# A pre-norm transformer block on one core: planner's places, warming products, the last attention unit and the closing sums of the last stage

## The chip, the cores and the metric

The kernel runs on one of the cores of a Trainium2 chip. The metric is the device time of one execution in microseconds (us). Besides the timed runs there is one profiled execution, whose trace the views of the profile are taken from. The core has five engines that each work through a list of their own in order: TensorE (PE; its weight loads are shown as PEld), VectorE (DVE), ScalarE (ACT), GpSimd (POOL) and SyncE (SP), which here only issues transfers. They wait for each other by semaphores.

## The reference

All is fp32. x has S = 2048 rows of D = 640; H = 32 heads of 20; F = 1728.

```python
x = A_x
h = x + attention(layernorm(x)) @ wo     # 32 heads, softmax over all 2048 keys, no mask
g = silu(layernorm(h) @ w_gate); u = layernorm(h) @ w_up
out = h + (g * u) @ w_down
```

Products are computed nearly exactly: each operand is split into a high part (type fp32r, one pass of PE) and a low part (the rest), and three of the four products of parts are added (`split`, L95 to L97: ScalarE rounds the high part, another engine subtracts).

## The kernel before, in words

**Start (to 17 us).** Four weight tiles and the first 512 rows of x are loaded. TensorE runs three fp32 products of no use as warming (L896 to L898), into a pair of banks that `ps_wide` (L80) takes in turn from three pairs (L74). VectorE normalises the rows (L755), TensorE transposes them (`flip_tokens`, L797) into pairs from the same turn, ScalarE and VectorE split them into z_hi and z_lo, and `first_blocks` (L819) multiplies the first two blocks of queries and keys into banks 0 and 1.

**Projections (to 336 us).** For four chunks c of 512 rows, ten blocks of queries and keys (`query_key`, two tiles of 128 columns a pair) and eight parts of values (`value`) are made. A product works on 64 rows, so that two of them, one in each half of the array, run side by side. In between stand row maxima of the attention scores that are computed early: score products against keys that have landed, with a maximum taken by VectorE. They give the largest score of each query, which the exponentials need. Two forms: `max_differences` (L200), two banks, where ScalarE writes the Relu of one half of the columns to a place in SBUF and VectorE adds and takes the maximum (L205, L207); and `max_twice` (L212), in two parts, where the first product's Relu is written to a place (L231) and the second product, issued later by the returned function, is added to it by VectorE (L224). The keys are first turned into differences by GpSimd (L431).

The order of all this is computed by the class `Halves` (L530) while the program is built. It keeps a modelled time for each half of PE, a time at which each engine is free (`use`), one for each of the eight banks (`places`), and issues what fits: `run` (L688) carries a block through both halves, `pair` (L605) puts in the next score product if a bank is free in the model, `finish_second` (L671) the second part of an open one. Before, each half can have one open product, and the three places for Relu (two halves of a spare query tile and a piece of v_stk, L512 to L520) are given out in rotation, whatever still reads them. `queries_at` (L994) is the modelled landing of a unit's queries, transfer plus 3.5 us. `raw_place` (L372) turns a weight tile that is no longer needed into a place for staged keys; ScalarE must once write it as fp32r from w_hi (L379), which `place` (L375) does; three of them are made at step 9 and one at step 6. `keep` (L833) splits a block and stores it.

**Attention (to 1476 us).** 32 units (8 groups of 4 heads, 4 chunks of queries) of 16 key tiles each. Per key tile TensorE makes four score products (`scores`, L1369), ScalarE four exponentials (L1380), and TensorE multiplies the probabilities by the values (`weigh`, L1382, eight instructions) one key tile later. A list `todo` holds the tiles whose weighing is due; a string of letters sets the order within a tile. In the last two units pieces of the output projection (`projection`, L1067) of the first two chunks are put in (`extra`): eight products of 128 x 320 (L1103), the moments, then four transposes (`flip`, L1128). By L1508 to L1510, unit 30 does the work of chunk 0 with whole rows (15 products of 128 rows), unit 31 that of chunk 1 with halved rows (`halved`, 30 products of 64 rows, into two banks, added by two operations of VectorE). In unit 31 the weighing is due two at a time on every second key tile up to tile 14 (L1472):

```python
both = u == NU - 1 and kt < NT - 1
for _ in range(2 * (1 - kt % 2) if both else 1):
    if todo:
        weigh_next()
```

**Feed-forward (to the end).** Two pairs of chunks, each over 14 blocks of F (`ELEMENTS`, L1342), by a Strassen-like scheme with seven instead of eight products. Element e runs in 6 or 8 steps (`step`); each step issues loads of weights from rings (`Ring`), some products of the down projection (`next_down`, L1646), prepares operands on GpSimd (`prepare`, `split` at L97, operand yp), and takes up to two `chores` (L2017). Chores are the closing sums of the scheme (`put_together`, L1673): 8 additions of 128 x 320 on GpSimd (L1684) for each of four token pairs of a pair of chunks. They have to be done before a token tile is stored; what is left of them then is issued at once (`plain`, L1687 to L1714). Elements 0 to 13 are of the first pair of chunks, 14 to 27 of the second, and the last blocks of the first pair's down projection run into elements 13 to 15. The last token tile is stored in two halves, both by SP (L1712).

## Time and profile before

| what | us |
|---|---|
| median of 3 runs | 2037.76 (2036.97 to 2040.04) |
| the profiled execution, its time | 2040.81 |
| its span, first to last instruction | 2039.0 |
| PE busy in the span | 2009.1 |
| VectorE, ScalarE, GpSimd busy | 1616.7, 1463.3, 778.5 |

"Busy" of PE is the union of modelled durations of its products, so a busy PE is not PE at its peak. The views used are the page (busy times, the chain of work that ended last), the table of windows (busy time by engine in stretches of the span, with the clock that TensorE was granted as a share of full speed), the list of waits (engine, line, what it waited for: us in total, times, longest), the groups by line, and the timeline (start, duration, engine, line, operation, tiles, number of instructions merged, and in brackets the idle time before and what ended it).

### The profile page before, as it was taken

The page shows a single profiled execution, that of the slowest core. Times are in us where ns is not written, and L with a number is a line of the kernel's source. Part 1 is how long each engine was busy: PE and PEld are TensorE (multiplying, and loading weights), DVE is VectorE, ACT ScalarE, POOL GpSimd, SP SyncE. Part 2 cuts the span into 40 slices and gives each one's busy share as a digit, 9 for nine tenths or more (in the row PEclk, how much of TensorE's full clock was granted, in tenths as well). Part 3 has the DMA queues.
Part 4 walks back from the last instruction along what each step waited for, and adds up shares of the span by engine and source line. Part 5 has one row for each costly group of instructions (what it writes and reads, how often), then busy time and mean ns, then how long its engine had stood idle before and what let it go on. Part 6 is the DMA issues. An engine that isn't in the chain of part 4 may idle for free.

```text
span 2039.0 us, 39356 instructions
## 1 busy us (share of the span) xinstructions
PE 2009.1 (99%) x13836; PEld 1244.3 (61%) x13836; DVE 1616.7 (79%) x3261; ACT 1463.3 (72%) x2948; POOL 778.5 (38%) x1075
## 2 busy tenths in 40 slices
PE   7999999999999999999999999999999999999998
PEld 6888897333333333333333333345598888888888
DVE  7769776888888888888888888886478666676677
ACT  4887887999999999999999999996634222212221
POOL 4464342234343434344430011001146454754555
PEclk9999999999999999999999999999999999999999
DMA  7775574343533534444433123211159654974642
GB/s 228 236 214 184 167 215 116 104 137 103 150 125 108 158 112 143 135 145 137 149 127 108 30 61 83 82 62 49 36 180 325 208 193 154 350 267 158 204 149 92
DMA packets 205206, 304.93 MB, mean 150 GB/s; under 512 B 47648, under 2 KB 82720, under 8 KB 203984
## 3 DMA queue, kind: packets, MB, share of 16 engines
q1 hardware_dynamic: 204912, 302.40, 45.6%
q8 instruction: 110, 1.80, 0.4%
q14 instruction: 88, 0.72, 0.1%
q10 hardware_dynamic: 96, 0.00, 0.0%
HBM read 205.78 MB, written 95.68 MB: 148 GB/s over the span
## 4 chain that ended last, share of the span: by engine, by line
PE 94%; DMA 2%; DVE 1%; ACT 1%; POOL 1%; issue 1%; SPq 0%; DVEq 0%; ACTq 0%; POOLq 0%
PE banks L1384 25%; PE banks L1374 17%; PE banks L1552 16%; PE banks L238 12%; PE banks L1646 8%; PE banks L569 8%; PE banks L1103 3%; PE banks L217 3%; PE banks L194 1%; DMA qk_d<-e 0%; PE banks L826 0%; PE banks L263 0%; DMA q_stk<-qk_d 0%; ACT q_stk L231 0%; DMA xt<-in_A_x 0%
## 5 line engine op out<-in xcount | busy, mean ns | idle before, releaser
L1380 ACT ACTIVATE probs<-banks 128x512 f32<-128x512 f32 x2048 | 1056.2, 614 | 61.1 <-PE banks L1374 25.3
L244 DVE TENSOR_REDUCE mx<-banks 128x1 f32<-128x512 f32 x1472 | 925.4, 684 | 124.9 <-PE banks L238 76.3
L1374 PE MATMUL banks<-q_stk,k_stk 62*128 62x512 f32 x2048 | 583.2, 428 | 1.5 <-ACT probs L1380 1.5
L1384 PE MATMUL banks<-probs,v_stk 128*32 128x512 f32 x4096 | 545.4, 606 | 0.0
L238 PE MATMUL banks<-k_stk,q_stk 60*128 60x512 f32 x1472 | 486.7, 438 | 0.2
L1374 PEld LDWEIGHTS banks<-q_stk,k_stk 62*128 62x128 f32 x2048 | 291.8, 184 | 283.7 <-ACT probs L1380 271.4
L238 PEld LDWEIGHTS banks<-k_stk,q_stk 60*128 60x128 f32 x1472 | 244.2, 184 | 163.1 <-DVE mx L244 126.8
L1769 DVE TENSOR_TENSOR tmp<-banks,tmp 128x512 f32<-128x512 f32 x208 | 141.2, 689 | 118.4 <-PE banks L1552 92.8
L1384 PEld LDWEIGHTS banks<-probs,v_stk 128*32 128x32 f32 x4096 | 81.3, 108 | 183.1 <-issue 171.4
L1646 PE MATMUL banks<-halves,yp 128*128 128x320 f32 x1032 | 178.9, 308 | 1.4 <-POOL yp L97 1.2
L1646 PEld LDWEIGHTS banks<-halves,yp 128*128 128x128 f32 x1032 | 165.2, 188 | 17.4 <-POOL yp L97 1.5
L1552 PE MATMUL banks<-t,units 128*128 128x512 f32 x624 | 162.7, 396 | 0.1
L97 POOL TENSOR_TENSOR yp<-y,yp 128x256 fp32r<-128x256 f32 x96 | 60.3, 628 | 195.2 <-ACT yp L96 181.0
L1552 PE MATMUL banks<-z,units 128*128 128x512 f32 x516 | 133.8, 394 | 0.0
L255 POOL CAST both<-neg 128x16 fp32r<-128x16 f32 x32 | 6.6, 206 | 314.7 <-PE banks L1374 138.2
L1552 PEld LDWEIGHTS banks<-t,units 128*128 128x128 f32 x624 | 112.5, 188 | 18.9 <-DVE tmp L1769 0.3
L1651 DVE TENSOR_TENSOR h<-banks,h 128x320 f32<-128x320 f32 x248 | 110.0, 481 | 6.8 <-PE banks L1646 5.4
L224 DVE CUSTOM_DVE_ANT_0 q_stk<-banks,q_stk 128x512 f32<-128x512 f32 x139 | 92.7, 687 | 26.0 <-PE banks L217 13.2
L569 PE MATMUL banks<-z_hi,w_hi 64*128 64x512 f32 x380 | 102.4, 406 | 1.9 <-ACT z_hi L96 1.8
L569 PE MATMUL banks<-z_lo,w_hi 64*128 64x512 f32 x380 | 103.3, 395 | 0.0
L1552 PEld LDWEIGHTS banks<-z,units 128*128 128x128 f32 x516 | 93.1, 187 | 16.1 <-DVE tmp L1769 0.2
L96 ACT ACTIVATE yp<-tmp 128x512 fp32r<-128x512 f32 x40 | 25.3, 632 | 103.2 <-POOL tmp L1639 103.2
(213 smaller groups left out, 2960.9 us busy)
## 6 DMA issues: line engine op xcount, KB each, us to landing
units<-w_d SPq DMA_DIRECT2D x186, 256.0 KB
w_d<-stage SPq DMA_DIRECT2D x106, 256.0 KB
halves<-j_d SPq DMA_DIRECT2D x70, 320.0 KB
k_stk<-qk_d SPq DMA_DIRECT2D x116, 160.0 KB
j_d<-stage SPq DMA_DIRECT2D x42, 320.0 KB
q_stk<-qk_d SPq DMA_DIRECT2D x64, 160.0 KB
k_stk<-qk_d SPq DMA_DIRECT2D x116, 80.0 KB
rb<-r_d SPq DMA_DIRECT2D x32, 256.0 KB
```

What stands on the lines that cost most here:

```text
L217: nc.tensor.matmul(ps, q[rows, pair, t * P : (t + 1) * P], k[rows, pair, :], start=True, stop=True)
L224: nc.vector.tensor_tensor_reduce(out=place, in0=ps, in1=place, scale=1.0, scalar=LEAST, op0=ALU.add, op1=ALU.max, accum_out=mx[:, b, pair, ...
L238: nc.tensor.matmul(ps, queries[u][rows, pair, t * P : (t + 1) * P], keys[u // NC][rows, pair, kc * CH : (kc + 1) * CH], start=True, stop=True,
L244: nc.vector.tensor_reduce(mxs[u][:, b, pair, t, kc : kc + 1], ps, axis=AX.X, op=ALU.max)
L569: product = nc.tensor.matmul(job["ps"][:, :out], lhs, rhs, start=(half == 0 and i == 0), stop=(half == 1 and i == job["n"] - 1),)
L1374: nc.tensor.matmul(ps, keys[u // NC][rows, p, kt * P : (kt + 1) * P], queries[u][rows, p, :], start=True, stop=True,)
L1380: nc.scalar.activation(probs[p][:, b, :], ps, AF.Exp, scale=scale)
L1384: nc.tensor.matmul(acc[32 * j : 32 * j + 32, :], values[u // NC][:, kt, j * VW : j * VW + 32], probs[j // 2][:, j % 2, :], start=(kt == 0) ...
L1552: nc.tensor.matmul(ps.rearrange("p (t n) -> p t n", t=TPC), w[k][:, i], z[k][:, :, j], start=(first and m == 0), stop=(last and m == len(n ...
L1646: nc.tensor.matmul(ps, a, b, start=(n == 0), stop=(n == len(pairs) - 1))
L1651: nc.vector.tensor_tensor(out=h, in0=ps, in1=h, op=ALU.add)
L1769: add = lambda out, ps, x: nc.vector.tensor_tensor(out=out, in0=ps, in1=x, op=ALU.add)
```

## The change

- The pairs of banks in turn are four (0, 2, 4, 6) instead of three; two warming products instead of three; the first blocks go to banks 2 and 3.
- The places for Relu have a modelled time each: `free_place` gives the one that is free first, or none, and then `pair` issues nothing. Each half may have two open products (`OPEN`).
- `raw_place` is written by VectorE, and may be used from the modelled end of that.
- Modelled times: ScalarE's two parts in `keep` 0.62 and 0.54 instead of 0.5 each; queries land 4.5 us after their transfer instead of 3.5.
- In the last unit two weighings on every second key tile only up to tile 9, one each from tile 10 on; the projection of chunk 1 has whole rows.
- The closing sums go one per step up to element 14, two after that.
- The first half of the last token tile is stored by ScalarE's queue.

```diff
-    wide_places, one_places = [2, 4, 6], []
+    wide_places, one_places = [0, 2, 4, 6], []
...
         def raw_place():
-            return place(raw_tile().rearrange("p a b -> p (a b)")[:, : 2 * CH], nc.scalar)
+            return place(raw_tile().rearrange("p a b -> p (a b)")[:, : 2 * CH], nc.vector)
...
-            if engine is nc.scalar:
+            if engine is nc.vector:
                 some = w_hi.rearrange("p k c -> p (k c)")[:, : 2 * CH].bitcast(F32)
-                nc.scalar.activation(t, some, AF.Copy)
-                pe.use("scalar", 1.0)
-                return t.rearrange("p (h n) -> p h n", h=2)
+                nc.vector.tensor_copy(t, some)
+                t = t.rearrange("p (h n) -> p h n", h=2)
+                place_at[id(t)] = pe.use("vector", 0.65) + 0.2
+                return t
...
-        def next_place():
-            relus.append(relus.pop(0))
-            return relus[-1]
+        relu_at = {}
+
+        def free_place(at):
+            place = min(relus, key=lambda r: relu_at.get(id(r), 0.0))
+            return place if relu_at.get(id(place), 0.0) <= at else None
...
-                self.second = [None, None]
+                self.second = [], []
...
-                if half is None and any(self.second) or half is not None and self.second[half]:
+                if half is None and any(self.second) or half is not None and len(self.second[half]) == OPEN:
                     return False
                 at = self.banks(1 if half is not None else 2)
                 if at is None:
                     return False
-                second = queue.pop(ahead)[1](at)
+                place = free_place(t + 0.43)
+                if place is None:
+                    return False
+                second = queue.pop(ahead)[1](at, place)
+                relu_at[id(place)] = math.inf
                 if half is not None:
                     start = self.stream(half, 0.231)
                     seen = self.use("scalar", 0.48, start + 0.43) + 0.2
                     self.places[at[0]] = seen
-                    self.second[half] = second, seen
+                    self.second[half].append((second, seen, place))
                     return True
...
                 for i, end in zip(at, ends):
                     self.places[i] = self.use("vector", 0.36, end) + 0.14
+                relu_at[id(place)] = self.places[at[1]]
                 return True
...
-                second, seen = self.second[half]
+                second, seen, place = self.second[half][0]
                 at = self.banks(1)
                 if at is None or self.now() + 0.43 < seen:
                     return False
-                self.second[half] = None
+                del self.second[half][0]
                 second(at)
                 start = self.stream(half, 0.231)
                 self.places[at[0]] = self.use("vector", 0.62, max(seen, start + 0.43)) + 0.14
+                relu_at[id(place)] = self.places[at[0]]
                 return True
...
-            pss = ps_at(range(2))
+            pss = ps_at((2, 3))
...
-                free = pe.use("scalar", 0.5, start)
-                done = pe.use("scalar", 0.5)
+                free = pe.use("scalar", 0.62, start)
+                done = pe.use("scalar", 0.54)
...
-        for _ in range(3):
+        for _ in range(2):
             nc.tensor.matmul(warm[:, 0], ident, xs[TPC - 1][:, :CH], start=True, stop=True)
...
-                    queries_at[u] = pe.sp(n=4, kb=750) + 3.5
+                    queries_at[u] = pe.sp(n=4, kb=750) + 4.5
...
-                    both = u == NU - 1 and kt < NT - 1
+                    both = u == NU - 1 and kt < NT // 2 + 2
...
                     ahead = projection(
-                        c - 1, ps_max if c < NC - 1 else (lambda: ps_b()), c == NC - 2
+                        c - 1, ps_max if c < NC - 1 else (lambda: ps_b())
                     )
...
-                nc.sync.dma_start(out[tt * P : (tt + 1) * P, cs], h_c[self.c][:, self.t + i, cs])
+                queue = nc.scalar if first and not half else nc.sync
+                queue.dma_start(out[tt * P : (tt + 1) * P, cs], h_c[self.c][:, self.t + i, cs])
...
-            for _ in range(2):
+            for _ in range(1 if e <= NF else 2):
                 if chores:
                     chores.pop(0)[2]()
```

More of the change, by code (lines that the diff above doesn't have):

```diff
@@ L41 @@
 MARGIN = 0.2
+OPEN = 2
 BEHIND = 2
@@ L452, in staged_keys, with one @@
                 all_products = [(t, pair, None) for t in range(TPC) for pair in range(2)]
-            def one(t, pair, b, at):
+            def one(t, pair, b, at, place):
                 rows = queries[u] if q is None else items[q][3]
                 if b is None:
-                    max_differences(mxs[u], rows, items[ks[0]][3], pair, t, kc, next_place(), at)
+                    max_differences(mxs[u], rows, items[ks[0]][3], pair, t, kc, place, at)
                     return over()
                 first, more = (items[k][3] for k in ks)
-                second = max_twice(mxs[u], rows, first, more, pair, t, kc, b, next_place(), at)
+                second = max_twice(mxs[u], rows, first, more, pair, t, kc, b, place, at)
                 return lambda at: (second(at), over())
@@ L482, in staged_keys @@
                     and (q is not None or pe.now() >= queries_at.get(u, math.inf)),
-                    lambda at, a=a: one(*a, at), a[2],
+                    lambda at, place, a=a: one(*a, at, place), a[2],
                 )
@@ L830, in first_blocks @@
             for m, ps in enumerate(pss):
-                pe.places[m] = keep(0, m, ps)
+                pe.places[2 + m] = keep(0, m, ps)
         def keep(c, m, ps):
```

## The prediction

> **What bounds the kernel now.** I read the page first, then a table of windows over the stages, then the waits of TensorE (PE), and the timeline only where PE waits.
>
> ```profile
> span 2039.0 us, 39356 instructions
> PE 2009.1 (99%) x13836; PEld 1244.3 (61%) x13836; DVE 1616.7 (79%) x3261; ACT 1463.3 (72%) x2948; POOL 778.5 (38%) x1075
> PE 94%; DMA 2%; DVE 1%; ACT 1%; POOL 1%; issue 1%; SPq 0%; DVEq 0%; ACTq 0%; POOLq 0%
> ...
> 13.00:325.00 312.00, 298.98 (x2744) 276.85 (x2744) 238.46 (x834) 247.29 (x537) 142.62 (x118) 0.98 0.65 201
> 1454.90:1476.40 21.50, 20.45 (x117) 7.54 (x113) 10.22 (x26) 14.76 (x29) 1.54 (x1) 0.92 0.00 1
> 1755.00:1795.00 40.00, 38.78 (x205) 33.99 (x204) 25.73 (x50) 7.41 (x15) 38.09 (x46) 1.00 0.99 369
> ```
>
> A row of windows gives stretch and length, then busy time of PE, weight loads, VectorE (DVE), ScalarE (ACT), GpSimd (POOL), then the granted clock. PE is nearly always busy and carries 94% of the chain, so only time in which PE stands still, or runs at a lower clock, can be won. Such time lies in four places: the first 17 us; the projections (13 of 312 us idle, clock 0.98); the last attention unit, whose closing 21.5 us have clock 0.92 and an ACT with 6.7 us to spare; and 1755 to 1795, where POOL is full and PE loses 1.2 us. The attention between has no edit.
>
> **Start: one warming product fewer, transposes spread over four pairs of banks.**
>
> ```profile
> 7.68 5.36 PE L898 MATMUL banks<-xt,ident 128*128 128x512 f32 x6 [7.68 <-DMA xt<-in_A_x]
> 11.07 1.66 DVE L755 TENSOR_SCALAR xt<-xt,mv,r_a 128x640 f32<-128x640 f32 x3
> 12.88 1.80 PE L801 MATMUL banks<-ident,xt 128*128 128x128 f32 x15
> 13.08 0.61 DVE L755 TENSOR_SCALAR xt<-xt,mv,r_a 128x640 f32<-128x640 f32 x1 [0.35 <-PE banks L898]
> 13.62 1.90 ACT L96 ACTIVATE z_hi<-banks 128x640 fp32r<-128x640 f32 x3 [2.86 <-PE banks L801]
> 15.24 0.77 PE L801 MATMUL banks<-ident,xt 128*128 128x128 f32 x5 [0.56 <-DVE z_lo L97]
> 16.80 2.58 PE L826 MATMUL banks<-z_hi,w_hi 128*128 128x512 f32 x10 [0.79 <-ACT z_hi L96]
> 5.98:9.39 3.41, 1.71 (x2) 0.84 (x3) 2.49 (x9) 0.00 (x0) 2.44 (x1) 1.00 1.04 363
> 9.39:12.80 3.41, 3.41 (x5) 1.25 (x4) 3.03 (x12) 1.36 (x2) 0.00 (x0) 1.00 1.10 350
> ```
>
> Three fp32 products are six instructions: (12.80 - 7.68) / 6 = 0.853 us each. Two products end at 11.1. The first tile is normalised at 11.07 + 0.55 = 11.6, so its transposes start near 11.8 instead of 12.88, and the fourth tile no longer waits 0.35 for the warming product that reads it. The fourth tile's transposes now go to banks 0 and 1, last used by the warming products, and lose the 0.56 behind VectorE. First conversion on ACT then at about 13.05; four of 0.63 follow without the present hole, so they end near 15.6 and L826 starts at 15.75 instead of 16.80: **1.0 us**. The first blocks' new banks 2 and 3 are those of the first tile, whose second part on DVE is over by 14.6: nothing. Bounds: 1.4 gained if the transposes are fast from their start, 1.7 lost if the clock rises later (a rival below).
>
> **Projections: the planner.** Here the order of instructions is computed from modelled times, and PE executes it strictly, so each wait is a place where the model was too early.
>
> ```profile
> PE banks L217 <- ACT q_stk L231: 4.3, 5, 1.6
> PE banks L217 <- ACT v_stk L231: 1.2, 1, 1.2
> PE banks L783 <- DVE mx L207: 1.7, 1, 1.7
> PE banks L194 <- DMA q_stk<-qk_d: 1.3, 2, 1.0
> ...
> 172.21 1.21 ACT L231 ACTIVATE q_stk<-banks 128x512 f32<-128x512 f32 x2 [1.98 <-DVE mx L224]
> 56.56 2.93 ACT L379 ACTIVATE raw<-w_hi 128x1024 fp32r<-128x1024 f32 x3
> 59.79 0.42 DVE L207 CUSTOM_DVE_ANT_0 v_stk<-banks,v_stk 128x256 f32<-128x256 f32 x1 [5.30 <-ACT v_stk L205]
> 46.94:50.35 3.41, 3.41 (x18) 3.09 (x20) 2.75 (x9) 1.99 (x6) 0.58 (x1) 0.50 0.59 179
> 60.59:64.00 3.41, 3.37 (x23) 3.28 (x25) 1.57 (x9) 3.35 (x10) 1.65 (x2) 0.50 0.59 210
> 173.23:176.64 3.41, 3.41 (x20) 3.16 (x18) 3.04 (x13) 1.72 (x4) 0.00 (x0) 0.50 0.31 118
> ```
>
> The first four rows are waits (total us, times, longest). Three causes, each met by an edit:
> - 4.3 + 1.2 = **5.5 us** behind L231: ACT writes its Relu into one of three places used in rotation, and stands (1.98 at 172.21) until DVE's L224 has read the old content; PE's next product then lacks its bank. Places chosen by modelled time, and a product held back while none is free, remove this kind of wait. How often the model is right no row shows: from 0 to 5.5. I take the middle, 2.7. Two open products per half change the order, not the work.
> - **1.7 us** at 60: three copies of 0.98 on ACT (L379) keep its evacuations back, and DVE idles 5.30. On DVE a 128x1024 copy should take 0.55 x 1024/640 = 0.9 (from L755). But DVE is slowed beside POOL:
>
> ```profile
> 41.16 2.11 DVE L755 TENSOR_SCALAR xt<-xt,mv,r_a 128x640 f32<-128x640 f32 x2
> 55.52 1.29 POOL L97 TENSOR_TENSOR v_stk<-v_stk 128x512 fp32r<-128x512 f32 x1 [2.05 <-ACT v_stk L96]
> ```
>
> Two such operations took 1.06 each beside a POOL instruction, and POOL is busy from 55.52 on, so the copies may end anywhere between 57.2 and 59.7; DVE's maxima queue behind them. I take 1.0 (bounds 0 and 1.7). The Trainium skill (SBUF — State Buffer, "Who interferes with whom") says why: a copy in a two-port mode and a POOL instruction exclude each other for a whole instruction; by that the copies wait out POOL's and the gain would be near 0.5; the row above agrees that DVE waits.
> - **1.3 us** at 46: PE reaches the first unit's products before its queries landed. One more us of margin: 1.0 (bounds 0 and 1.3).
> - Each of the three longest stands is followed by a window of 3.41 us at clock 0.50, worth half of it, 1.7: 5.1 in all. I take two of three as gone: 3.4 (bounds 0 and 5.1). The truer ScalarE times in keep belong to the same account.
> - A new order brings new waits, which no row of before shows. The nearest rows are the present ones, some 1.2 each; I charge two, 2.5 (bounds 0 and all that is won).
>
> Sum: 2.7 + 1.0 + 1.0 + 3.4 - 2.5 = **5.6 us**, between 0 and 13.6. Held-back products find room at the end:
>
> ```profile
> 324.50:336.00 11.50, 11.06 (x119) 10.62 (x116) 0.89 (x6) 3.24 (x9) 0.80 (x1) 1.00 0.63 168
> L224 DVE CUSTOM_DVE_ANT_0 q_stk<-banks,q_stk 128x512 f32<-128x512 f32 x139 | 92.7, 687 | 26.0 <-PE banks L217 13.2 <-PE banks L569 8.2 <-ACT q_stk L231 3.7
> ```
>
> In these last 11.5 us PE runs projections and DVE works for 0.89; a maximum costs DVE 0.69, so some 15 products that were held back fit there free.
>
> **Last unit: weighing once per key tile from tile 10 on, whole rows.**
>
> ```profile
> 1418.71 0.77 PE L1135 MATMUL banks<-ident,z 128*128 128x128 f32 x5
> 1421.28 0.76 PE L1135 MATMUL banks<-ident,z 128*128 128x128 f32 x5
> 1458.01 1.92 PE L1384 MATMUL banks<-probs,v_stk 128*32 128x512 f32 x16
> 1462.93 3.17 PE L1384 MATMUL banks<-probs,v_stk 128*32 128x512 f32 x16
> 1460.39 4.03 ACT L1380 ACTIVATE probs<-banks 128x512 f32<-128x512 f32 x8 [0.90 <-PE banks L1374]
> ...
> 1423.95 2.42 PE banks L1103 x30
> 1398.97 2.41 PE banks L1103 x15
> ```
>
> Now PE issues the scores of two tiles, then weighs two (1.92) while ACT, done with eight exponentials, runs dry (0.90 here); one weighing ran at the low clock (3.17). With one weighing per tile the cadence is that of the unit before: 1421.28 - 1418.71 = 2.57 per tile with a flip. From 1458.01, where tiles 9 and 10 have their scores: a weighing, 0.96; tile 11, half of 4.03 of exponentials and a weighing, 3.0; four tiles with flips, 4 x 2.6 = 10.4; two weighings left over after the loop instead of one, 1.9; 0.3 for the last exponential. End at 1474.6 against 1476.4, where the row of windows ends: **1.8 us** (bounds: -1.0, if only the extra weighing shows, and 4.0). Whole rows halve the instructions (15 for 30) at the same stream: 2.41 against 2.42, so PE gains **0**; eight additions less on DVE lie beside PE. Bounds: the length of a product, 2.41 / 15 = 0.16, gained or lost at each of eight changes to the scores, 1.3 either way.
>
> **Last stage.**
>
> ```profile
> PE banks L1646 <- POOL yp L97: 1.2, 1, 1.2
> L1684 POOL TENSOR_TENSOR h<-h,own 128x320 f32<-128x320 f32 x20 | 18.1, 909 | 1.2
> ...
> 2031.69 2.69 DVE L1651 TENSOR_TENSOR h<-banks,h 128x320 f32<-128x320 f32 x6
> L1712 SPq DMA_DIRECT2D out<-h x17: 332/383/1062, 1781.2 to 2034.6; - x17
> ```
>
> The 32 closing sums take 32 x 0.909 = 29.1 of POOL's 38.09 us in this window; the splits that PE needs queue behind them, and PE waits once, 1.2. At one per step they spread over twice the time, POOL has some 14 us to spare: **1.2 us**. What is late next: sums left over are flushed, up to eight (7 us), before a tile's store, and SP's later loads queue behind that store; the weights already in the rings cover that. If they don't, a stand like the present one returns; so 0 to 1.2. At the end the last store issues at 2034.6, 0.2 after its addition ended (2031.69 + 2.69), because SP is still issuing the one before; ScalarE's queue takes that one: **0.2 us** (0 if its issue is as slow).
>
> **Sum:** 1.0 + 5.6 + 1.8 + 0 + 1.2 + 0.2 = 9.8 us. The profiled execution took 2040.8 (span 2039.0), 3.0 above the median of the runs, 2037.8; its waits are of the same kind, so I take the sum from the median: **2028.0 us**.
>
> **Rivals.**
> - New waits eat all that the planner wins. For it: every instruction of 300 us is placed anew. Against it: five of the present waits share one cause that is now modelled. Left are 1.0 + 1.8 + 1.2 + 0.2: 2037.8 - 4.2 = 2033.6.
> - The clock stays low at the start. In the rows above, a window with 1.71 of 3.41 us busy did not raise it, the full one did; two products fill 3.41 us, one window only if they begin with it. Then the first blocks run a window at half clock, 1.7 lost, and the 1.0 is not won: 2028.0 + 2.7 = 2030.7. The Trainium skill (TensorE: Matmul & The Clock Gate, Part 1) states that window, free-running, and Part 4 adds that transposes do not count as busy; by that this is the usual case, while the trace leaves open whether 0.5 or 1.0 of a window is needed.
> - Slower: products held back for want of a place (three places, up to four open products) pile up past the stage's end, where PE waits for DVE. It decides from 15 on; each further one costs 0.69. To turn 9.8 us won into 4.2 lost takes 20 more, 35 of the 208 products of this kind (139 in the row and 69 in its sister): 2042 or above.
> - The order hardly changes and the edits cancel: 2037.
>
> **Chances.** Forecast 0.50, new waits 0.18, low clock 0.14, slower 0.12, no effect 0.06. A measurement of this kernel tells about 0.2%, 4.1 us, from no change. Faster: 0.50 + 0.14 + half of 0.18 = 0.73; same: 0.09 + 0.06 = 0.15; slower 0.12. The range goes from 2019 (nearly all of the 13.6 won, 4.0 in the last unit) to 2038 (all cases but the slower one).
>
> **What would show it.** Right: L826 starts near 15.8; waits of PE on L231 below 3 us and no L379 on ACT; at most one window at 0.50 before 330; the last weighing ends 2 us earlier counted from the unit's start; no wait on POOL yp. Wrong: L217 or L194 products after the last L569, a first block at half clock, or a wait of PE on DMA in 1780 to 1830.

## The result, and the profile after

The changed kernel takes 2026.36 us (median of 4 runs, 2025.38 to 2028.81) against 2038.62 (2036.97 to 2040.04) of the kernel before in the same comparison: ratio 0.9944, 95% interval 0.993 to 0.9957. The forecast was 2028.0. The profiled executions differ by more, 2026.52 against 2040.81, 14.3 us. The kernel before was timed again with each group of runs below (medians 2036.84 to 2039.15), so kernels of different groups are compared by their ratios to it.

The page of the changed kernel, its span, busy times and chain of work:

```profile
span 2024.7 us, 39120 instructions
...
PE 2002.5 (99%) x13714; PEld 1237.8 (61%) x13714; DVE 1620.2 (80%) x3257; ACT 1460.2 (72%) x2944; POOL 779.8 (39%) x1075
...
PE 95%; DVE 2%; ACT 1%; issue 1%; POOL 1%; DMA 0%; SPq 0%; ACTq 0%; DVEq 0%; POOLq 0%
```

PE still sets the time: it is busy for 6.6 us less in a span that is 14.3 shorter, so more than half of what was won is time in which it stood still.

Now the same stages, cut at their own first and last products, first of the kernel before, then of the changed one (stretch and length; busy time of PE, weight loads, DVE, ACT, POOL; granted clock). The rows are the projections, the last unit's key tiles 0 to 8, its tiles from 9 to the last weighing, and a stretch with the closing sums:

```profile
16.80:334.35 317.55, 305.89 (x2825) 284.23 (x2826) 236.27 (x833) 246.58 (x537) 142.62 (x118) 0.98 0.66 202
1421.98:1454.93 32.95, 32.95 (x349) 24.17 (x348) 14.35 (x35) 22.04 (x43) 5.97 (x4) 1.00 0.19 55
1454.93:1476.44 21.51, 20.46 (x117) 7.58 (x113) 10.23 (x27) 14.76 (x29) 1.54 (x1) 0.92 0.00 1
```

```profile
15.30:323.38 308.08, 302.18 (x2824) 279.59 (x2825) 242.67 (x837) 243.18 (x533) 141.84 (x118) 1.00 0.67 209
1411.20:1445.04 33.84, 33.84 (x230) 22.32 (x229) 10.78 (x29) 21.95 (x43) 6.00 (x4) 1.00 0.18 53
1445.04:1462.94 17.90, 17.45 (x117) 6.80 (x113) 10.35 (x26) 14.94 (x30) 1.56 (x1) 1.00 0.00 1
1742.00:1786.00 44.00, 44.00 (x234) 38.68 (x233) 28.83 (x55) 8.02 (x16) 38.03 (x46) 1.00 0.99 365
```

The projections are 9.5 us shorter: PE stands still for 5.9 instead of 11.7, and the clock is 1.00 instead of 0.98 (three windows at 0.50 before, none now). In the last unit the first nine tiles are 0.9 longer and the rest 3.6 shorter. With the closing sums POOL has 6 us to spare in 44, and PE none idle. In full, by such marks:

| stretch | change, us | forecast |
|---|---|---|
| first transfer lands (no edit) | -0.5 | 0 |
| first warming product to first block | -1.0 | -1.0 |
| projections | -9.5 | -5.6 |
| units 0 to 30 | +0.2 | 0 |
| last unit, tiles 0 to 8 (whole rows) | +0.9 | 0 |
| last unit, tile 9 to the last weighing | -3.6 | -1.8 |
| last weighing to the feed-forward | +0.8 | 0 |
| feed-forward | -1.7 | -1.2 |
| last product to the end (ScalarE's store) | +0.1 | -0.2 |

The +0.8 holds a wait of 0.7 us behind ACT's o_hi, in the projection that follows the unit. It does not come from the change: over the fourteen profiles of this document this stretch takes 18.5 to 19.4 us, and 19.4 in two kernels that weigh in twos to tile 14. The -0.5 is chance as well: the first transfer lands at 7.2 to 8.7 us. The total agrees with the forecast better than its parts do, and that is luck in part: terms that were too small and terms that were too large offset each other, as told further down.

### The profile page after: what moved, and what is told of

Read it like the earlier page. It is cut to its first block, busy times and chain, and to the rows that moved or that the text cites. A ratio compares the mean times of both kernels' runs of the same rounds, so it can differ in the third digit from the quotient of the medians.

```text
span 2024.7 us, 39120 instructions
## 1 busy us (share of the span) xinstructions
PE 2002.5 (99%) x13714; PEld 1237.8 (61%) x13714; DVE 1620.2 (80%) x3257; ACT 1460.2 (72%) x2944; POOL 779.8 (39%) x1075
## 3 DMA queue, kind: packets, MB, share of 16 engines
q8 instruction: 109, 1.79, 0.4%
## 4 chain that ended last, share of the span: by engine, by line
PE 95%; DVE 2%; ACT 1%; issue 1%; POOL 1%; DMA 0%; SPq 0%; ACTq 0%; DVEq 0%; POOLq 0%
PE banks L1394 25%; PE banks L1384 17%; PE banks L1562 17%; PE banks L239 12%; PE banks L573 9%; PE banks L1656 8%; PE banks L1113 3%; PE banks L218 3%; PE banks L195 1%; PE banks L836 0%; PE banks L264 0%; DVE st L133 0%; DMA o_t<-o_d 0%; PE banks L1145 0%; PE banks L793 0%
## 5 line engine op out<-in xcount | busy, mean ns | idle before, releaser
L1562 PEld LDWEIGHTS banks<-t,units 128*128 128x128 f32 x624 | 112.5, 188 | 18.9 <-DVE tmp L1780 0.4
L573 PE MATMUL banks<-z_hi,w_hi 64*128 64x512 f32 x380 | 105.6, 396 | 2.3 <-ACT z_hi L97 2.0
L573 PE MATMUL banks<-z_lo,w_hi 64*128 64x512 f32 x380 | 105.2, 393 | 0.0
L573 PE MATMUL banks<-z_hi,w_lo 64*128 64x512 f32 x380 | 101.8, 391 | 0.0
```

The lines of the kernel that those rows point to most:

```text
L573: product = nc.tensor.matmul(job["ps"][:, :out], lhs, rhs, start=(half == 0 and i == 0), stop=(half == 1 and i == job["n"] - 1),)
L1562: nc.tensor.matmul(ps.rearrange("p (t n) -> p t n", t=TPC), w[k][:, i], z[k][:, :, j], start=(first and m == 0), stop=(last and m == len(n ...
```

## The experiments

My theory after the result: the modelled places take away the waits behind L231, and the low clock with them, and that is nearly all of the projections' gain; weighing once per tile and the spread of the closing sums carry the rest; whole rows cost. The rival: an order that is computed anew hits or misses its waits by luck, so that any edit to the model would have shuffled them as well. Twelve kernels tell these apart.

### One edit alone on the kernel before: places, copies, margin

The first has the modelled places with one open product per half, and nothing else of the change; the second only raw_place on VectorE; the third only the margin of the queries.

```diff
+OPEN = 1
...
-        def next_place():
-            relus.append(relus.pop(0))
-            return relus[-1]
+        def free_place(at):
+            place = min(relus, key=lambda r: relu_at.get(id(r), 0.0))
+            return place if relu_at.get(id(place), 0.0) <= at else None
...
```

> The kernel before, with only the modelled places for the Relu (one open product per half as before). The projections are measured from the first block (L826, 16.8 us in the trace of before) to the first score product of the attention (334.4): 317.6 us; in the changed kernel 308.1. Theory A (the gain is the sum of the waits that each edit removes, and of the low-clock windows behind them): the waits of PE on L231, 5.5 us, fall below 2, the low-clock window at 173 goes, 1.7; the waits at 46 and 60 and their two windows stay. Projections 311 to 314 us, the whole 3 to 6 us faster than before. Theory B (any new order by the planner is as good as a throw of dice; the changed one happened to be good): waits of PE on ScalarE and VectorE in all still 5 us or more, projections within 2 us of 317.6 or longer.

Measured: 2028.81 us (2026.85 to 2031.44), ratio 0.9945 (0.9927 to 0.9963); the projections take 305.09 us, 3.0 less than with the whole change and some 6 less than Theory A's least. Its waits of PE between 13 and 330 us (us in total, times, longest), the largest two, and its row of the projections:

```profile
PE banks L792 <- DVE mx L208: 1.6, 1, 1.6
PE banks L572 <- DVE mx L208: 1.4, 1, 1.4
```

```profile
16.59:321.68 305.09, 299.38 (x2825) 278.18 (x2826) 238.20 (x834) 244.53 (x537) 140.16 (x117) 0.99 0.68 211
```

No wait of PE behind a Relu (L231 before, L232 after) is left in the whole list; it was 5.5 us. The wait at 60 us (1.6 here) and a low-clock window behind it are still there, as Theory A says. The places alone give the time of the whole change. Of the 12.5 us that they win in the projections, 6.0 are standing time of PE (5.7 instead of 11.7) and about 3.4 are two low-clock windows less (one instead of three). The last 3 us lie in PE's busy time: the same products, and more of them side by side. No list of waits shows that part.

```diff
-            return place(raw_tile().rearrange("p a b -> p (a b)")[:, : 2 * CH], nc.scalar)
+            return place(raw_tile().rearrange("p a b -> p (a b)")[:, : 2 * CH], nc.vector)
```

> The kernel before, with only the places for staged keys written by VectorE instead of ScalarE. Theory A: the wait of 1.65 at 60 goes and the low-clock window behind it, 1.7; the rest of the order is nearly that of before; projections 314 to 315.5 us against 317.6, the whole 2 to 3.5 us faster. Theory B: the wait goes but others of the same sum appear elsewhere, projections within 1 us of 317.6.

Measured: 2043.15 us (2041.69 to 2045.43), ratio 1.0022 (1.0013 to 1.0032), 0.2% longer; projections 317.80 against 317.55. The largest waits of PE between 13 and 330 us:

```profile
PE banks L217 <- ACT q_stk L231: 3.4, 4, 1.4
PE banks L570 <- ACT z_hi L96: 2.0, 3, 0.9
```

```diff
-                    queries_at[u] = pe.sp(n=4, kb=750) + 3.5
+                    queries_at[u] = pe.sp(n=4, kb=750) + 4.5
```

> The kernel before, with only the margin for the landing of the queries 4.5 instead of 3.5 us. Theory A: the wait of 1.35 at 46 goes and the low-clock window behind it, 1.7; projections 314.5 to 316 us against 317.6, the whole 1.5 to 3 us faster. Theory B: within 1 us of 317.6, by new waits elsewhere.

Measured: 2042.45 us (2038.98 to 2046.18), ratio 1.0016 (1.0007 to 1.0025), 0.2% longer; projections 317.92. The largest wait:

```profile
PE banks L217 <- ACT v_stk L231: 3.0, 2, 2.1
```

Each edit removes the wait it was made for: the 1.7 us of PE behind L207 at 60 us is gone from the one list, the 1.3 behind the queries' transfer from the other. But the waits behind L231 are still there, and with the margin one of them is 2.1 long. Waits are not the whole of it, though. The rows of the projections, with the copies and then with the margin:

```profile
17.59:335.39 317.80, 309.80 (x2824) 283.79 (x2825) 239.72 (x836) 242.88 (x533) 142.94 (x119) 0.99 0.65 202
```

```profile
15.72:333.64 317.92, 308.38 (x2824) 281.99 (x2825) 235.92 (x832) 245.73 (x537) 142.38 (x119) 0.99 0.65 202
```

PE stands for 8.0 and 9.5 us instead of 11.7, and there is one low-clock window instead of three; and yet the stage is no shorter, since PE is busy for 309.8 and 308.4 us instead of 305.9. The products are as many and, at full clock, as long as before, so fewer of them run side by side in the new order; why is not shown. Here the rival has a point: an edit to the model draws another order of 300 us, and that alone is worth several us either way. But it does not explain the places, which remove a kind of wait of PE in every order that has them.

### What the second open product, the copies, the margin and keep are worth beside the places

The changed kernel with one open product per half:

```diff
-OPEN = 2
+OPEN = 1
```

> The changed kernel with one open product per half instead of two. Theory A (the modelled places do the work, a second open product only alters the order): projections within 1 us of the 308.1 of the changed kernel. Rival: the second open product is what lets PE go on while a place is being read; without it the products are held back longer, and projections take 2 us or more longer, waits of PE on ScalarE and VectorE back above 5 us.

Measured: 2029.06 us (2028.18 to 2030.66), ratio 0.995 (0.9935 to 0.9965); projections 308.98, as Theory A says. The end of its projections on PE (start, duration, line, number of products):

```profile
318.47 2.57 PE L195 MATMUL banks<-raw,xt 60*128 60x512 f32 x7
321.27 3.55 PE L195 MATMUL banks<-raw,xt 60*128 60x512 f32 x9 [0.23 <-DVE mx L225]
324.37 1.14 PE L1384 MATMUL banks<-q_stk,k_stk 62*128 62x512 f32 x2
```

From 318.47 to 324.37 PE has only score products left, and goes at the pace of the maxima: 0.37 us from one product to the next, where the three products just before took 0.23. At 321.6 the clock falls to 0.50, and it stays there for 10.24 us, into the attention. That is the mechanism of the rival "slower": products pile up at the stage's end. It is real, and costs a few us, not 14: some 2 us by the pace, and units 0 to 30 take 1.9 more than in the changed kernel.

Then the other way round, from below. The base is the kernel before with all edits of the change but four: one open product, halved rows, raw_place on ScalarE with the old margin, and keep's modelled times of ScalarE as they were (0.5 and 0.5).

```diff
-OPEN = 2
+OPEN = 1
...
-                free = pe.use("scalar", 0.62, start)
-                done = pe.use("scalar", 0.54)
+                free = pe.use("scalar", 0.5, start)
+                done = pe.use("scalar", 0.5)
...
-                        c - 1, ps_max if c < NC - 1 else (lambda: ps_b())
+                        c - 1, ps_max if c < NC - 1 else (lambda: ps_b()), c == NC - 2
```

> The planner of the run with the modelled places alone (one open product, staged places written by ScalarE, the old margin and the old times of keep), with the changed kernel's start, weighing, closing sums and store, and halved rows. The projections took 305.1 us there and 308.1 in the changed kernel, measured from the first block; halved rows 0.9 less. Theory A (the stages add up): 2026.4 - 3.0 - 0.9 = 2022.5 us, between 2020 and 2024.5. Theory B (the planner's order is a throw of dice, and the new start throws anew): projections anywhere between 305 and 318, the whole between 2022 and 2035.

Measured: **2022.62 us** (2021.51 to 2023.39), ratio 0.9918 (0.9904 to 0.9931): as Theory A says, and less than both kernels, though its interval just touches that of the changed kernel (0.993 to 0.9957). Projections 305.02. To it the copies and the margin were added, and in another kernel the second open product:

```diff
-                    queries_at[u] = pe.sp(n=4, kb=750) + 3.5
+                    queries_at[u] = pe.sp(n=4, kb=750) + 4.5
...
-                nc.scalar.activation(t, some, AF.Copy)
+                nc.vector.tensor_copy(t, some)
```

> The version with modelled places, one open product and halved rows (2022.62 us, projections 305.0), with the copies of raw_place on VectorE and 4.5 us of landing for the queries added. Theory A (the modelled places are the whole gain of the projections; these two edits only move waits): projections 305 plus or minus 1.5, time 2021.5 to 2024. Theory B (their 3.7 us of the first 50 us, seen when each was made alone on the kernel before, come on top once no wait behind rotated places can give them back): projections 301.5, time 2019. Theory C (they move score products to the end of the stage, where the last maxima pile up): projections 309, as in the changed kernel with one open product, a last early maximum less than 1 us before the stage's end, time 2026.

Measured: 2023.19 us (2021.6 to 2023.89), ratio 0.9934 (0.9922 to 0.9947); projections 304.65.

```diff
-OPEN = 1
+OPEN = 2
```

> The version with modelled places, one open product and halved rows, with two open products per half. Theory A (the second open product is worth nothing here, the modelled places alone are): projections 305 plus or minus 1.5, time 2021.5 to 2024. Theory B (it is what makes the changed kernel's projections 308 instead of 305): 307 to 309, time 2025 to 2027. Theory C (it helps): 303 or less.

Measured: 2023.74 us (2023.05 to 2024.22), ratio 0.9938 (0.9925 to 0.995); projections 304.39. Theory A both times: beside the places, neither the copies and the margin nor the second open product move the projections by more than 0.7 us. The total of these two does not stand clear of the changed kernel's ratio; the projections do.

This leaves one edit for the difference between 305 and what the changed kernel has. The changed kernel with one open product and the base with copies and margin differ, up to the attention, in the two numbers of keep alone: 308.98 against 304.65. And all profiles agree: with keep's new times the projections took 308.1 to 315.1 us in seven kernels (308.08, 308.98, 309.07, 309.12, 311.07, 313.72, 315.14), with the old ones and modelled places 304.4 to 305.1 in four. The new times are truer: in these traces the two parts take 1.26 us from the first's start to the second's end, and the model has 1.16 instead of 1.0. They cost at least 3 us in both orders that have them. But the seven kernels share only these two orders, and the four share three; that every order with the new times would lose is not shown. Here are the last 11.5 us of the projections, of the base with copies and margin and of the changed kernel:

```profile
308.50:319.95 11.45, 11.45 (x120) 11.40 (x117) 6.27 (x34) 6.30 (x20) 0.00 (x0) 1.00 0.38 121
```

```profile
312.00:323.40 11.40, 11.40 (x112) 10.98 (x110) 10.05 (x45) 9.73 (x26) 0.00 (x0) 1.00 0.62 202
```

DVE is busy for 6.27 us in the one and 10.05 in the other (2.33 in the kernel before, cut at the same distance; the prediction's row, with 0.89, reached 1.65 us into the attention): the order with the new times keeps more of its score products for the end. What that costs the rows do not show, since PE is busy throughout in both. The changed kernel's largest waits of PE between 13 and 330 us are:

```profile
PE banks L573 <- ACT z_hi L97: 2.0, 2, 1.1
PE banks L218 <- DVE mx L225: 1.5, 1, 1.5
PE banks L573 <- DVE mx L225: 1.2, 1, 1.2
```

The base with copies and margin has 1.3 and 1.2 in place of the first two and nothing in place of the third: 2.2 of the 3.4 us between the two kernels; the rest lies in PE's busy time. That keep's times were not put back alone, in the kernel with two open products, is the one step missing here.

### Last unit: whole rows, weighing

The changed kernel with halved rows again in the last unit:

```diff
-                        c - 1, ps_max if c < NC - 1 else (lambda: ps_b())
+                        c - 1, ps_max if c < NC - 1 else (lambda: ps_b()), c == NC - 2
```

> The changed kernel with halved rows in the last unit again (30 products of 64 rows, two banks, two additions). The eight projections lie between the first scores of tiles 0 and 9 of that unit: 32.95 us in the trace of before, 33.84 in the changed kernel and 33.82 in the run with one open product. Theory A (whole rows cost PE time: a change between products of 128 rows and scores of 62 rows keeps both halves waiting for each other): 32.9 to 33.1 us, the whole 0.8 to 1.0 us faster than the changed kernel. Rival (the 0.9 us come from the other edits of the unit or from chance): 33.8 us and no gain.

Measured: 2027.86 us (2023.99 to 2036.51, 6 runs), ratio 0.995 (0.9931 to 0.9969). From the unit's first scores to those of tile 9 it takes 32.95 us instead of 33.84. The projection's first products in two successive pairs of tiles, of the changed kernel and then of this one:

```profile
1413.11 1.00 PE L1113 MATMUL banks<-wo_hi,o_hi 128*128 128x320 f32 x5
...
1421.09 1.00 PE L1113 MATMUL banks<-wo_hi,o_hi 128*128 128x320 f32 x5
```

```profile
1438.77 1.00 PE L1113 MATMUL banks<-wo_hi,o_hi 64*128 64x320 f32 x10
...
1446.52 1.00 PE L1113 MATMUL banks<-wo_hi,o_hi 64*128 64x320 f32 x10
```

7.98 us from one to the next with whole rows, 7.75 with halved ones, with the same products of the attention between them: 0.23 four times over is the 0.9. In all fourteen profiles this stretch is 32.9 to 33.0 with halved rows and 33.8 to 33.9 with whole ones. The total does not show it: the runs of this kernel spread over 12.5 us, and the profiled one lost 7 us in its projections, told below.

The changed kernel with weighings in twos to tile 14 again:

```diff
-                    both = u == NU - 1 and kt < NT // 2 + 2
+                    both = u == NU - 1 and kt < NT - 1
```

> The changed kernel with two weighings on every second key tile up to tile 14 again. From the first scores of tile 9 to the end of the last weighing it is 21.5 us in before (one low-clock window in it), 17.9 in the changed kernel (none), 18.9 in the run with one open product (one). Theory A (weighing in twos lets ScalarE run dry, whatever the clock): 19.8 without a low-clock window, 21.5 with one, 23 with two; the whole 2 to 5 us slower than the changed kernel. Rival (the gain is only the low-clock window, which comes or stays away by chance): within 1 us of 17.9 where no window falls, 18.9 to 19.5 with one.

Measured: 2031.06 us (2028.84 to 2033.01), ratio 0.9958 (0.9943 to 0.9974). From tile 9 to the last weighing 23.17 us with two low-clock windows, as Theory A says; the total does not stand clear of the changed kernel's. Two weighings of this kernel, the first in such a window and the second at full clock:

```profile
1455.85 3.49 PE L1394 MATMUL banks<-probs,v_stk 128*32 128x512 f32 x16
1463.12 1.92 PE L1394 MATMUL banks<-probs,v_stk 128*32 128x512 f32 x16
```

The stretch has few lengths over the fourteen profiles. In twos: 21.4 to 21.5 with one low window (three kernels), 23.2 with two (two kernels); a window is worth 1.7 there, so with none it would be some 19.8, an estimate. One per tile: 17.9 with none (six kernels), 18.9 with one (three kernels). So the cadence itself is worth an estimated 1.9 us, and the low window of the trace of before, which that of after lacks, the rest of the 3.6. In twos there are 1.4 such windows on average, one per tile 0.3; whether the cadence brings them is not shown.

### Last stage: two closing sums per step

```diff
-            for _ in range(1 if e <= NF else 2):
+            for _ in range(2):
```

> The changed kernel with two closing sums per step in the first pair again. From the first product of the feed-forward stage to the last it is 538.9 us in before and 537.2 in the changed kernel. Theory A: the wait of PE on GpSimd's yp, 1.2 us, comes back, and the stage is 538.4 to 538.9 us; the whole 1.2 to 1.7 us slower. Rival (the wait moves or is covered): 537.2 to 537.6 us.

Measured: 2028.27 us (2024.81 to 2032.05), ratio 0.9945 (0.9926 to 0.9965); feed-forward 539.04 us, 1.8 more than in the changed kernel, while the total does not show it (ratio 0.9944 there). Its waits of PE in that stage:

```profile
PE banks L1656 <- POOL yp L98: 1.3, 1, 1.3
PE banks L1656 <- DVE h L1661: 0.2, 1, 0.2
```

The stand behind POOL is back at its old price of 1.2 to 1.3. The changed kernel's list for the stage has only the second line. The half us beyond the stand may be chance: over the fourteen profiles the stage takes 538.8 to 539.0 with two sums per step (five kernels) and 537.2 to 538.3 with one (nine), 1.3 to 1.4 apart by their means.

### Start: three warming products, and one

```diff
-        for _ in range(2):
+        for _ in range(3):
```

> The changed kernel with three warming products instead of two. Theory A (a warming product that is left out shortens the start): each costs 0.85 us in the row of before, the transposes wait for the third, and first warming product to first block becomes about 8.9 us (9.12 before, 7.25 to 8.09 in the kernels with two); the stages behind do not change, so the time goes up by about 1. Theory B (what shortens the start are the four pairs of banks, and the warming products lie beside the normalising): 8.1 us again.

Measured: 2027.73 us (2026.71 to 2032.66), ratio 0.9959 (0.9944 to 0.9974). First warming product to first block: 7.97 us (8.09 in the changed kernel, 9.12 before). The start on PE of the changed kernel, then of this one:

```profile
7.21 3.75 PE L908 MATMUL banks<-xt,ident 128*128 128x512 f32 x4 [7.21 <-DMA xt<-in_A_x]
11.13 3.28 PE L811 MATMUL banks<-ident,xt 128*128 128x128 f32 x20 [0.17 <-DVE xt L765]
15.30 2.57 PE L836 MATMUL banks<-z_hi,w_hi 128*128 128x512 f32 x10 [0.89 <-ACT z_hi L97]
```

```profile
8.28 4.84 PE L908 MATMUL banks<-xt,ident 128*128 128x512 f32 x6 [8.28 <-DMA xt<-in_A_x]
12.96 2.35 PE L811 MATMUL banks<-ident,xt 128*128 128x128 f32 x20
16.25 2.56 PE L836 MATMUL banks<-z_hi,w_hi 128*128 128x512 f32 x10 [0.94 <-ACT z_hi L97]
```

Theory B by the number; the total is not clear of the changed kernel's. The third product takes 1.1 us, and the transposes get it back by running at full pace from the first on (2.35 for twenty, against 3.28). But that pace is not the third product's doing. It comes when the clock rises, 12.97 us in the changed kernel, among its transposes, and 12.36 here, ahead of them; and in five of the eight kernels with two products the transposes take 2.40 to 2.55. In both the 20 transposes are one run without a stand, where before there were 15, a hole of 0.56 behind VectorE, and 5. So the four pairs of banks shorten the start. But one start varies: eight kernels with two products and four pairs need 7.25 to 8.1 us (mean 7.56), four with three products and three pairs 8.3 to 9.6 (mean 8.90). By these means the whole is 1.3, of which this kernel leaves the product 0.4, with one profile to go by: between 0 and 0.7.

```diff
-        for _ in range(2):
+        for _ in range(1):
```

> The changed kernel with one warming product. Theory A (one is enough, since the first tile is normalised 3.9 us after the first product began, whatever TensorE does): first warming product to first block 7.3 to 8.1 us as with two, first block 2.57 us for ten instructions. Theory B (low clock): TensorE then stands between the warming product and the transposes, no window of 3.41 us is filled, the transposes and the first ten instructions run at the low clock (first block 3.5 to 5.1 us), and the projections' end comes 1 to 3 us later than with two.

Measured: 2030.21 us (2026.0 to 2035.35, 10 runs), ratio 0.997 (0.9958 to 0.9981). First warming product to first block 8.73 us.

```profile
7.58 2.05 PE L908 MATMUL banks<-xt,ident 128*128 128x512 f32 x2 [7.58 <-DMA xt<-in_A_x]
11.56 3.90 PE L811 MATMUL banks<-ident,xt 128*128 128x128 f32 x20 [1.94 <-DVE xt L765]
16.31 2.60 PE L836 MATMUL banks<-z_hi,w_hi 128*128 128x512 f32 x10 [0.84 <-ACT z_hi L97]
```

Half of Theory B: PE stands for 1.94, most transposes run at the low clock (median 421 ns against 273 before), and that costs 0.6 against the changed kernel, up to 1.5 against the quickest starts. But the clock is up before the first block, whose ten products take 2.60 as always. By this one profile two products are enough, and one nearly so. The rest of the difference in time lies in the projections (311.07), as told next.

### One order, 308 to 315 us

The changed kernel and the five kernels that undo only its warming, last unit or sums issue the same products in the same order in the projections, and yet these took 308.08, 309.07, 309.12, 311.07, 313.72 and, with halved rows, 315.14 us. Most of the spread is low clock: the first two have none of it in this stage, the third one window of 3.41 us, the next two a stretch of 6.83 each, and the last one of 17.07, of which 10.35 lie in the projections. At half the clock that costs up to 1.7, 3.4, 3.4 and 5.2 us; without it the six lie at 307.4 to 310.3. Two waits of ACT ahead of such stretches, first in the kernel with three warming products, then in that with halved rows, here with the wait of PE that followed:

```profile
226.38 0.60 ACT L352 ACTIVATE e<-banks 128x512 f32<-128x512 f32 x1 [1.83 <-DMA qk_d<-e]
```

```profile
319.71 0.44 ACT L883 ACTIVATE ev<-banks 128x320 f32<-128x320 f32 x1 [2.24 <-DMA v_d<-ev]
...
320.20 0.49 PE L195 MATMUL banks<-xt 60*128 60x512 f32 x1 [2.01 <-ACT ev L883]
```

The stretch at low clock behind the latter; the former is followed by one from 227.4 on:

```profile
321.10:338.10 17.00, 16.78 (x68) 13.12 (x68) 7.56 (x33) 9.62 (x24) 5.15 (x2) 0.50 0.28 100
```

ACT can't evacuate a block because its buffer's last contents are still on their way to memory; its queue stands, in the latter kernel PE stands 2.01 behind it, and then the clock falls to 0.50. The changed kernel's timed runs spread over 3.4 us, those of the five relatives over 4 to 13; those of the three kernels built up from below, with keep's old times, over 1.2 to 2.3. But the order with one open product and the new times spreads over 2.5, and the places alone, with the old ones, over 4.6, with 4 to 10 runs each. That the new times make an order depend more on when a store lands is a guess.

## Why the prediction was right, and where not

**Projections: right in kind, mis-sized (5.6, measured 9.5).** The relu term was the mis-sized one: of 5.5 us behind L231 I took the middle, 2.7, because no row told how often the model would be right. PE no longer pays for it: in the eleven kernels with modelled places one wait of PE behind a Relu is left, of 0.2 us. But the model is not right. The Relu itself still stands on ACT until VectorE has read its place, 7.4 us instead of 9.0; the waits of ACT between 13 and 330 us, before and then after:

```profile
ACT q_stk L231 <- DVE mx L224: 7.0, 6, 2.0
ACT v_stk L231 <- DVE mx L224: 2.0, 2, 1.3
```

```profile
ACT q_stk L232 <- DVE mx L225: 4.7, 6, 2.9
ACT v_stk L232 <- DVE mx L225: 2.7, 3, 1.7
```

With keep's old times it is 1.0 to 5.3 us in four kernels, with the new ones 4.7 to 7.4 in seven. Why PE gets by without waiting for these Relus is not shown.

The low clock was taken at two windows of three, and all three went in the trace of after (clock 1.00). That is luck in part: four of the five relatives with the same order have low clock in this stage, and over the six it takes 2.3 us on average, against 5.1 in the trace of before. The terms for the copies (1.0) and the margin (1.0) were wrong as terms: alone each made the kernel 0.2% longer, and beside the places they are worth at most 0.4 us together. They take away the waits that I named, and the new order costs as much in PE's busy time; a sum of waits removed does not hold when the order is computed anew. The 2.5 for new waits was near, if the changed kernel's waits of L573 behind VectorE and of L218 (2.7) are counted as the new ones. What I had put beside them as "the same account", keep's truer times, is the edit that loses: at least 3 us in the orders tried.

**Last unit, weighing: 1.8 right for the cadence (an estimated 1.9).** Another 1.7 came from the low window, which I had seen in the row (3.17) and not charged.

**Whole rows: 0 was wrong, 0.9 lost.** I had set the stream, 2.41 against 2.42, against the stream. Undoing this edit alone gives the 0.9 back. PE has no standing time in either row, so the cost must lie at the eight changes between the projection and the attention's products, some 0.11 each if they share it evenly; I had bounded it at 0.16 and then left it out of the sum.

**Closing sums: right** (1.2 forecast, the stand itself 1.2 to 1.3; the flush did not bring a new one). **Start: right sum, half wrong reason.** The 1.0 is there, but the kernel with three products has it too: the banks give most of it. I had counted a product as 0.85 us ahead of the transposes; by the means it is worth 0.4. Nor had I asked when the clock rises, which sets the pace of the transposes.

**ScalarE's store: 0.2 forecast, nothing measured.** From the last addition's end to the end of the span it took 4.6 us before (2034.4 to 2039.0) and 4.7 after (2020.0 to 2024.7). The store of the last half now issues at once, and what is waited for is its landing.

**The rivals.** The signs named for being right all came, and none of those for being wrong. New waits did not eat the gain, but four of the six kernels with the change's order show a low-clock stretch in the projections that the changed kernel's own trace lacks. Low clock at the start: it did not stay low. The prediction left open how full a window must be: with one open product a window with PE busy for 2.85 of 3.41 us raised the clock (7.58 to 10.99), and with the copies alone one with 2.61 did not (7.24 to 10.65). The Trainium skill (TensorE: Matmul & The Clock Gate, Part 4) says that products in transpose mode do not count as busy in the same way. With one warming product the clock came up at 14.68 us, behind a window in which PE did nothing but these transposes, after a stand of 1.94 us; so for them, which the trace lists as plain MATMUL, it does not bear that out. Products piled up at the end: shown, in the kernel with one open product, at a few us, where 14 were needed for the slower side.

## What to carry to other kernels

When an order is computed from modelled times, first model the resource whose waits come most often (here three places used in rotation); here, correcting single times without that won nothing, and with it next to nothing. A truer duration in such a model can make the order worse: look what it pushes to the end of the stage, and try each number by itself. Every edit to the model draws a new order, so read PE's busy time beside its waits, and profile more than one execution of an order before a difference of a few us is called an edit's. And price the joints, the changes between two kinds of products, as well as the streams.

## What the runs showed of the hardware

**The clock falls without an idle window.** In the middle of these kernels the clock fell to 0.50 on 23 occasions in fourteen profiles: 19 times for 3.41 us, and four times for two, three or five times as long. Each came behind a window of 3.41 us in which PE was busy for 1.4 to 2.97 us. In the last unit 0.45 us of standing was enough; the row is the window ahead of the one at 1463.5 in the kernel before:

```profile
1460.09:1463.50 3.41, 2.96 (x16) 1.07 (x18) 0.00 (x0) 3.11 (x7) 0.00 (x0) 1.00 0.00 0
```

The Trainium skill (TensorE: Matmul & The Clock Gate, Part 1) has the window, 3413 ns and free-running, and says that the clock goes back after an idle one. The length agrees; that it takes an idle window does not: none of these was idle. Busy time alone does not decide it: with the places alone, a window with PE busy for 2.00 us (97.5 to 100.91) kept the full clock, and with halved rows PE was busy throughout from 321.1 to 331.3 and the clock stayed at 0.50. What decides was not tried.

**A copy on VectorE waits out a GpSimd instruction.** The copies of 128 x 1024 for raw_place took 0.69 us each, and 1.79 for the last, which ran into GpSimd's at 50.11 us. The changed kernel's copies (least, median and longest in ns) and that instruction:

```profile
L380 DVE CAST raw<-w_hi x4: 686/686/1786, 39.0 to 50.2; 128x1024 fp32r<-128x1024 f32 x4
```

```profile
50.11 1.36 POOL L98 TENSOR_TENSOR z_lo<-xt,z_hi 128x512 fp32r<-128x512 f32 x1 [2.03 <-ACT z_hi L97]
```

The extra 1.10 is about what was left of that 1.36, and in all nine kernels that copy on VectorE the last copy took 1.77 to 1.79. The Trainium skill (SBUF — State Buffer, "Who interferes with whom") says that the later of two such instructions blocks wholly; this agrees. ScalarE took 1.04 for such a copy, with nobody in its way.
